# The split of the values moved from VectorE to GpSimd, from the third pair of heads on

## The chip, the cores and the metric

The kernel runs on one core of one Trainium2 chip. The metric is the time of one execution on the device in microseconds (us). Before the change the median of three runs is 1172.41 us (1171.74 to 1175.49).

A core has five engines, each with a queue of instructions of its own that it works off in order: TensorE (PE in the profile; PEld is its loading of weights), VectorE (DVE), ScalarE (ACT), GpSimd (POOL) and SyncE (SP), which here issues nearly all transfers (DMAs). Engines wait for one another by semaphores. SBUF is the memory on the core, with 128 partitions; PSUM is where TensorE puts its sums.

## The reference

Attention with pooled queries, then a mixture of experts in which each token goes to one expert. Cut to what matters:

```python
# q, k, v: (8, 8, 1152, 64) float32
q_pool = q.reshape(B, H, S // 2, 2, D).mean(axis=3)          # 576 queries
scores = (1 / np.sqrt(D)) * q_pool @ k.transpose(0, 1, 3, 2)
scores = scores - scores.max(-1, keepdims=True)
attn = np.exp(scores)
attn = attn / (attn.sum(-1, keepdims=True) + 1e-9)
x = (attn @ v).transpose(0, 2, 1, 3).reshape(4608, 512)

logits = x @ w_gate + modality_bias[modality_id]             # 8 experts
e_idx = logits.argmax(1)
probs = softmax(logits)
for e in range(8):                                           # w1[e]: 512 x 1024, w2[e]: 1024 x 512
    mask = e_idx == e
    out[mask] = probs[mask, e][:, None] * (np.maximum(x[mask] @ w1[e], 0) @ w2[e])
```

## The kernel before

The 64 heads are worked on as 32 pairs: two batches of one head, one in the lower and one in the upper 64 partitions. To keep nearly float32 precision on float16 matrix products, each operand is split into a high part (the value rounded to float16) and a low part (the remainder, again float16), and products of the parts are summed in PSUM.

A loop runs over 576 steps, 18 for each pair. In each step a fixed string of letters says how much of each kind of work is put out: matrix products for the row maxima (`maxpass`, a pair ahead), scores and exponentials (`scores`), products of exponentials and values (`pv`). Everything that prepares a pair is put at a step relative to its first one, by constants such as `T_QH`, `T_VH` or `T_VL`. So the order of instructions on TensorE, VectorE, ScalarE and GpSimd is written out by hand (`MANUAL`). SyncE is not in that list: the order of its transfers is set by a planner when the program is made, from what it expects to be ready when.

What the engines do for a pair `p`, with the lines of the profile:

- *Queries and keys.* GpSimd adds the two queries of each pool (L613, `rawq<-rawq`), rounds them to `qh` (L620) and forms the remainders of queries and keys (L648, `lo`); ScalarE rounds the keys to `hi` (L632). SyncE then moves `qh` into `QB`, for the maxima, and `qh`, `lo` and `hi` into the operands `B` (L583), and loads the next `rawq`, `rawk` and `rawv` (L598, L599, L603).
- *Maxima.* TensorE multiplies `QB` and `hi` into `pm`, in one of three PSUM buffers (L781, L789); VectorE reduces each to its maximum (L782, L790), forms `m` (L753), TensorE turns it (L757), VectorE writes it as a row `mr` (L766), and SyncE moves the row into `B` (L767).
- *Scores.* TensorE makes the scores (L843, L844), ScalarE the exponentials as 32 bit words (`Pe`, L845). The upper halves of these words are the high parts; the lower halves are turned into the low parts `Pl` by ScalarE for two thirds (L826) and by VectorE for one (L828).
- *Values.* ScalarE sums the squares of the pair's values (L694), TensorE adds over the partitions (L700), and VectorE makes of it a power of two, the scale `sc` (L708). Then the function `values` runs four times a pair, with `PARTS` cutting nine chunks of 128 keys into five and four (640 and 512 columns). With `lo` false, GpSimd writes the scaled values, rounded to float16, into `VH` (L735); with `lo` true, VectorE computes value times scale minus `VH` into `vl` in one instruction (L733). Their steps are 15 and 14 ahead of the pair (the piece of 512 first) and 11 and 2 ahead. VectorE also makes `VS`, which is `VH` times 2^-16 (L745, 12 steps ahead). `VH` and `VS` have three buffers each, by the pair's number, and `vl` three.
- *Products.* TensorE multiplies `VH`, `vl` and `VS` with the parts of the exponentials into `xp` (L894, L895, L896). VectorE divides by the sums and writes `x` (L912, L913, L917). After each odd pair SyncE stores the 128 columns of the two (`xs<-x`, L218), and ScalarE and VectorE split them (L862, L869) for the logits.

The first two pairs differ: there GpSimd scales the values in place (L730) and subtracts (L731), after ScalarE has made `VH` (L737). After each eight pairs VectorE and GpSimd route the tokens of two batches (`route`); in the last pairs VectorE also makes the lists of tokens for the first expert blocks (`first_list`). After about 760 us come the expert layers, in which VectorE and ScalarE split the weights and GpSimd gathers and scatters tokens.

The function that the change touches and what calls it:

Of the kernel before, what the change touches and what calls it, by code (L numbers as in the profile page):

```python
# [16 lines left out]
ALU = mybir.AluOpType  # L17
# [62 lines left out]
QH_POOL = True  # L80
LO_POOL = (0, 1, 2)
VH_POOL = (0, 1)
EV_ACT = ()
IN_PM = (0, 1, 2, 3, 4, 5)
EVD = 1
# [463 lines left out]
def attention(tc, ctx, att, ident, npairs, xpool, on_two, on_split, on_scale, jobs, side, set_pm, started, ahead, hip):  # L549
# [3 lines left out]
    nc = tc.nc  # L553
# [25 lines left out]
    def need(p, *names):  # L579
        assert all((p, n) in made for n in names), f"pair {p}: {names} are not made yet"  # L580
# [137 lines left out]
    flat = lambda a: a.rearrange("p c j d -> p (c j) d")  # L718

    def values(p, i, lo):  # L720

        s = st[p]
        c = slice(*PARTS[lo][i:i + 2])
        made.add((p, f"v{'hl'[lo]}{i}"))
        if lo:
            need(p, f"vh{i}")
        v = flat(s["v"].rearrange("p (c j d) -> p c j d", c=NKC, j=2)[:, c])
        vh = flat(VH[p % 3][:, c, :, 0:D])
        if lo and p < 2:
            nc.gpsimd.tensor_scalar(v, v, s["sc"], None, op0=ALU.mult)  # L730
            nc.gpsimd.tensor_tensor(flat(s["vl"][:, c]), v, vh, op=ALU.subtract)  # L731
        elif lo:
            nc.vector.scalar_tensor_tensor(flat(s["vl"][:, c]), v, s["sc"], vh, op0=ALU.mult, op1=ALU.subtract)  # L733
        elif p > 1 and i in VH_POOL:
            nc.gpsimd.tensor_scalar(vh, v, s["sc"], None, op0=ALU.mult)  # L735
        else:
            nc.scalar.activation(vh, v, AF.Copy, scale=s["sc"])  # L737
# [283 lines left out]
    for p in range(npairs):  # L1021
        b = NSTEP * p
        go = lambda t, f, *a, p=p, b=b, **k: at(b + t, p, lambda: f(p, *a), **k)
        if p > 1:
            d = D2 if p == 2 else (0,) * 5
            go(T_K2 - b if p == 2 else T_KQ, load_kq, end=False)
            go(T_SPLIT + d[0], split_q)
            go(T_QH + d[1], split_qh)
            for i in range(2):
                go(T_HI[i] + d[2], split_hi, i)  # L1030
            for i in range(3 if LOC else 7):
                go(T_LO[LOCI[i] if LOC else i] + d[3], split_lo, i)
            go(T_MAX + d[4], lambda p: mxq.append(maxpass(p)), end=False)
            go(T_PLACE + (T_P2 if p == 2 else 0), place, end=False)
            go(T_LV, load_v)
        elif p:
            go(T_P1 - b, place, end=False)
            go(T_M1 - b, lambda p: mxq.append(maxpass(p)), end=False)
            go(T_LV, load_v)
        sq, power_, vh, vs, vl = (T_SQ, T_POW, T_VH, T_VS, T_VL) if p > 1 else V1 if p else V0  # L1040
        if p == 1:
            go = lambda t, f, *a, p=p: at(t, p, lambda: f(p, *a))
        go(sq, square)
        go(power_, power)
        for i, t in enumerate(vh):
            go(t, values, i, False)
        go(vs, shifted)
        for i, t in enumerate(vl):
            go(t, values, i, True)
# [15 lines left out]
    for t in range(NSTEP * npairs):  # L1065
        p, c18 = divmod(t, NSTEP)
# [422 lines left out]
```

## Time and profile before

The profile is one execution of the program, taken by the hardware profiler.

| What | Value |
|---|---|
| Median of three runs | 1172.41 us |
| The profiled execution's own time | 1171.42 us |
| Its span, first to last instruction | 1169.7 us |
| Busy: PE, DVE, ACT, POOL | 95%, 84%, 78%, 36% |
| Granted TensorE clock, mean | 0.996 |
| Products of values (L894), first and last start | 31.4 and 763.1 us |

How to read it: a row that names a line has engine, operation, what is written `<-` what is read, the shape, and how often (x). In a table of groups there follow the total busy time in us, the mean of one in ns, and the idle time of the engine just ahead of it with what ended it. In a view in order of time a row begins with the start and the length in us, and the bracket says how long the engine had been idle and for what it had waited; a row may merge neighbours of one form (x2). In a list of waits the three numbers are the total in us, how often, and the longest. A wait is put down to the semaphore that came last. Matrix products are pipelined and their ends modelled; the spans on POOL are rough.

### The profile page before, as it was taken

What the parts mean: (1) busy time and instruction counts of PE and PEld (TensorE: products, weight loads), DVE (VectorE), ACT (ScalarE), POOL (GpSimd) and SP (SyncE); (2) the same over time, 40 slices, a digit from 0 to 9 for tenths busy, and PEclk for the clock granted to TensorE, in tenths of its full rate; (3) what the DMA queues carried; (4) which work ended last, traced back from release to release, by engine and by line L of the source; (5) the groups of instructions that cost most, each with busy time, mean ns of one, the idle gap of its engine ahead of it and who ended that gap; (6) DMA issues with size and microseconds to landing.
All of it is one profiled execution on the core that took longest, in us unless ns stands there. A gap on an engine that the chain in (4) does not pass through costs nothing. (4 is left out here: it accounts for less than half of the span.)

```text
span 1169.7 us, 36628 instructions
## 1 busy us (share of the span) xinstructions
PE 1113.4 (95%) x14962; PEld 816.2 (70%) x14962; DVE 985.5 (84%) x2031; ACT 918.1 (78%) x1459; POOL 417.3 (36%) x393
## 2 busy tenths in 40 slices
PE   6989999999999999999999899999999999999995
PEld 2667777777777777777776677767667676676763
DVE  6898898999999999999999999888997757566661
ACT  5879999998999998999998888865466656566561
POOL 7743444444435344443444352123112121211200
PEclk9999999999999999999999999999999999999998
DMA  7667768767668678578577463499999999999970
GB/s 226 168 160 174 162 169 200 156 168 177 169 165 189 176 165 177 160 172 193 151 183 173 135 135 93 146 292 279 222 283 283 333 270 284 276 284 275 258 250 22
DMA packets 175569, 232.66 MB, mean 199 GB/s; under 512 B 92351, under 2 KB 126799, under 8 KB 175392
## 3 DMA queue, kind: packets, MB, share of 16 engines
q1 hardware_dynamic: 169254, 210.45, 69.4%
q0 software_dynamic: 6128, 19.78, 6.3%
q8 instruction: 119, 1.95, 0.7%
q14 instruction: 58, 0.48, 0.2%
q10 hardware_dynamic: 10, 0.00, 0.0%
HBM read 146.11 MB, written 19.18 MB: 141 GB/s over the span
## 5 line engine op out<-in xcount | busy, mean ns | idle before, releaser
L845 ACT ACTIVATE Pe<-psc 128x432 int32<-128x432 f32 x768 | 381.5, 527 | 65.1 <-PE psc L844 54.3
L782 DVE TENSOR_REDUCE mp<-pm 128x1 f32<-128x512 f32 x566 | 369.8, 683 | 13.7 <-PE pm L781 8.2
L894 PE MATMUL xp<-VH,Pe 128*128 128x65 f16 x2880 | 373.2, 193 | 0.0
L896 PE MATMUL xp<-VS,Pl 128*128 128x65 f16 x2880 | 372.6, 193 | 0.4 <-DVE Pl L828 0.4
L895 PE MATMUL xp<-vl,Pe 128*128 128x64 f16 x2880 | 371.3, 192 | 0.0
L895 PEld LDWEIGHTS <-Pe 128*128 128x128 f16 x2880 | 267.6, 98 | 87.8
L894 PEld LDWEIGHTS <-Pe 128*128 128x128 f16 x2880 | 272.1, 98 | 57.1 <-issue 19.4
L844 PE MATMUL psc<-B 65*128 65x432 f16 (+2 forms) x1152 | 306.7, 289 | 1.9 <-DMA B<-mr 1.8
L843 PE MATMUL psc<-B 128*128 128x432 f16 (+2 forms) x1152 | 306.0, 288 | 1.7 <-ACT Pe L845 1.7
L896 PEld LDWEIGHTS <-Pl 128*128 128x128 f16 x2880 | 266.4, 97 | 0.6 <-DVE Pl L828 0.5
L781 PE MATMUL pm<-hi,QB 128*128 128x512 f16 x566 | 215.4, 383 | 17.6 <-DVE mp L782 13.6
L826 ACT ACTIVATE Pl<-Pe 128x1152 f16<-128x1152 uint16 x186 | 216.5, 1164 | 5.9
L735 POOL TENSOR_SCALAR VH<-rawv,sc 128x512 f16<-128x512 f32 (+1 forms) x60 | 103.7, 1739 | 185.4 <-PE xp L896 125.4
L648 POOL TENSOR_TENSOR lo<-rawk,hi 128x576 f16<-128x576 f32 (+1 forms) x68 | 90.2, 1329 | 182.1 <-ACT hi L632 142.2
L1228 PE MATMUL ph<-xpart,w1h 128*128 128x256 f16 x544 | 148.3, 273 | 0.1
L1230 PE MATMUL ph<-xpart,w1l 128*128 128x256 f16 x544 | 148.3, 273 | 0.0
L1229 PE MATMUL ph<-xpart,w1h 128*128 128x256 f16 x544 | 148.3, 273 | 0.0
L844 PEld LDWEIGHTS <-B 65*128 65x128 f16 x1152 | 113.4, 98 | 25.8 <-issue 3.2
L843 PEld LDWEIGHTS <-B 128*128 128x128 f16 x1152 | 113.0, 98 | 9.0 <-issue 3.7
L828 DVE TENSOR_SCALAR Pl<-Pe 128x576 f16<-128x576 uint16 (+1 forms) x198 | 108.1, 546 | 8.5 <-ACT Pe L845 7.1
L1276 PE MATMUL po<-w2h,hl 128*128 128x512 f16 x296 | 112.2, 379 | 0.0
L1275 PE MATMUL po<-w2l,hh 128*128 128x512 f16 x296 | 112.2, 379 | 0.0
(263 smaller groups left out, 1790.6 us busy)
## 6 DMA issues: line engine op xcount, KB each, us to landing
w2r<-in_w_dram SPq DMA_DIRECT2D x76, 512.0 KB
w1r<-in_w_dram SPq DMA_DIRECT2D x72, 512.0 KB
rawv<-in_att_dram SPq DMA_DIRECT2D x32, 576.0 KB
B<-hi SPq DMA_DIRECT2D x128, 144.0 KB
rawq<-in_att_dram SPq DMA_DIRECT2D x31, 576.0 KB
rawk<-in_att_dram SPq DMA_DIRECT2D x31, 576.0 KB
B<-qh SPq DMA_DIRECT2D x128, 72.0 KB
B<-lo SPq DMA_DIRECT2D x64, 144.0 KB
```

The costliest lines, as they stand in the source:

```text
L781: nc.tensor.matmul(pm, QB[p % 2][:, u], s["hi"][:, t * 512:(t + 1) * 512], start=True, stop=True)
L782: nc.vector.tensor_reduce(mp[:, u, t:t + 1], pm, op=ALU.max, axis=AX.X)
L826: nc.scalar.activation(low, rest, AF.Copy, scale=LOW)
L843: nc.tensor.matmul(o, b1[:, ks], b1[:, qs], start=True, stop=False, skip_group_check=True)
L844: nc.tensor.matmul(o, b2[:, ks], b2[:, qs], start=False, stop=True, skip_group_check=True)
L845: nc.scalar.activation(Pe[:, D + x0:D + x1], pt, AF.Exp, scale=1.0 / 16)
L894: nc.tensor.matmul(out, Ph[:, qs], vh[:, c, j, 0:D + 1], start=c == 0 and g == 0, stop=False, skip_group_check=True)
L895: nc.tensor.matmul(out[:, 0:D], Ph[:, qs], vl[:, c, j], start=False, stop=False, skip_group_check=True)
L896: nc.tensor.matmul(out, Pl[:, qs], vs[:, c, j, 0:D + 1], start=False, stop=c == NKC - 1, skip_group_check=True)
L1228: nc.tensor.matmul(o, hi[:, c, fs], xh[:, :, c], start=c == 0, stop=False)
L1229: nc.tensor.matmul(o, hi[:, c, fs], xl[:, :, c], start=False, stop=False)
L1230: nc.tensor.matmul(o, lo[:, c, fs], xh[:, :, c], start=False, stop=c == 3)
```

## The change

From the third pair on (`VLP = 2`) `values` takes a new branch. With `lo` false, GpSimd multiplies the float32 values by the scale in place and then copies them to `VH`, which rounds them. With `lo` true, GpSimd subtracts `VH` from the scaled values and writes `vl`. The steps at which the function is called stay as they are; VectorE's instruction on L733 and GpSimd's on L735 are no longer reached.

```diff
+VLP = 2
...
         v = flat(s["v"].rearrange("p (c j d) -> p c j d", c=NKC, j=2)[:, c])
         vh = flat(VH[p % 3][:, c, :, 0:D])
-        if lo and p < 2:
+        if p >= VLP:
+            if lo:
+                nc.gpsimd.tensor_tensor(flat(s["vl"][:, c]), v, vh, op=ALU.subtract)
+            else:
+                nc.gpsimd.tensor_scalar(v, v, s["sc"], None, op0=ALU.mult)
+                nc.gpsimd.tensor_copy(vh, v)
+        elif lo and p < 2:
             nc.gpsimd.tensor_scalar(v, v, s["sc"], None, op0=ALU.mult)
             nc.gpsimd.tensor_tensor(flat(s["vl"][:, c]), v, vh, op=ALU.subtract)
         elif lo:
```

## The prediction

> **What bounds the kernel now.** I read the span on the page first, then the table of busy time by stretches, then who waited for whom on TensorE and VectorE, then the order of time of one pair, engine by engine.
>
> ```profile
> span 1169.7 us, 36628 instructions
> 60.00:560.00 500.00, 485.37 (x8333) 374.37 (x8331) 463.89 (x1041) 460.81 (x781) 217.17 (x175) 1.00 0.73 173
> 560.00:740.00 180.00, 168.72 (x2890) 129.39 (x2889) 173.07 (x420) 160.08 (x267) 66.58 (x53) 1.00 0.59 141
> 373.97:395.94 21.97, 21.97 (x390) 17.12 (x389) 21.46 (x48) 20.64 (x36) 9.68 (x7) 1.00 0.57 155
> ```
>
> The columns of the last three rows are the length, then busy PE, PEld, DVE, ACT, POOL, the granted clock and DMA. The change acts between 60 and 740 us. TensorE is idle there for 14.6 + 11.3 = 25.9 us, at a granted clock of 1.00. One whole pair (373.97 to 395.94) has TensorE busy from end to end: relieving VectorE gives nothing in such a pair. So the gain can come only from the idle time of TensorE. The next view says who ended it, first for 100 to 560 us, then for 560 to 740 us (total, times, longest).
>
> ```profile
> PE pm L781 <- DVE mp L782: 6.5, 10, 1.4
> PE pm L757 <- DVE m L753: 1.6, 3, 0.5
> ...
> PE pm L781 <- DVE mp L782: 6.1, 10, 1.0
> PE pm L757 <- DVE m L753: 2.5, 5, 1.0
> ```
>
> VectorE ends most of it: 8.1 us in the long middle and 8.6 us in the last seven pairs, where VectorE also makes the lists of tokens for the experts and is busy 173 of 180 us. These 16.7 us are the ceiling of a gain by VectorE. Part of the middle is no lack of VectorE at all, but a transfer that VectorE waits for, ahead of the maxima that TensorE needs:
>
> ```profile
> DVE x L917 <- DMA xs<-x: 18.5, 9, 2.9
> 411.90 0.55 DVE L917 SCALAR_TENSOR_TENSOR x<-xp,sc,rr 128x320 f32<-128x320 f32 x1 [2.06 <-DMA xs<-x]
> 413.10 0.38 PE L781 MATMUL pm<-hi,QB 128*128 128x512 f16 x1 [0.50 <-DVE mp L782]
> ```
>
> **The change, part by part.** VectorE loses two instructions in each of 30 pairs. GpSimd's two scalings turn into scalings in place, and gain two copies and two subtractions. The forms are all in the trace, some from the first two pairs, or at 576 columns:
>
> ```profile
> L733 DVE SCALAR_TENSOR_TENSOR vl<-rawv,sc,VH 128x640 f16<-128x640 f32 x30 | 28.3, 943 | 0.0
> L733 DVE SCALAR_TENSOR_TENSOR vl<-rawv,sc,VH 128x512 f16<-128x512 f32 x30 | 22.3, 744 | 0.0
> L730 POOL TENSOR_SCALAR rawv<-rawv,sc 128x640 f32<-128x640 f32 x2 | 4.1, 2038 | 7.7 <-ACT VH L737 4.5 <-issue 3.2
> L730 POOL TENSOR_SCALAR rawv<-rawv,sc 128x512 f32<-128x512 f32 x2 | 3.3, 1662 | 0.0
> L731 POOL TENSOR_TENSOR vl<-rawv,VH 128x640 f16<-128x640 f32 x2 | 2.9, 1460 | 0.2
> L731 POOL TENSOR_TENSOR vl<-rawv,VH 128x512 f16<-128x512 f32 x2 | 2.2, 1116 | 0.2
> L620 POOL CAST qh<-rawq 128x576 f16<-128x576 f32 x30 | 20.1, 670 | 0.1
> ```
>
> *Removed from VectorE*: 28.3 + 22.3 = 50.6 us, 1.69 us a pair.
>
> *Added to GpSimd*: the scalings in place cost 2.04 + 1.66 against 1.89 + 1.56 (the rows of one pair, below), so +0.25; two copies at 0.67 per 576 columns are 0.74 + 0.60; the subtractions are 1.46 + 1.12. Sum 4.17 us a pair, from 9.68 to 13.85 of 21.97 us. It has the room, but it is a queue in order, and here is where its pieces stand in one pair:
>
> ```profile
> 373.97 1.56 POOL L735 TENSOR_SCALAR VH<-rawv,sc 128x512 f16<-128x512 f32 x1 [5.58 <-PE xp L896]
> 375.51 1.89 POOL L735 TENSOR_SCALAR VH<-rawv,sc 128x640 f16<-128x640 f32 x1
> 377.34 0.67 POOL L620 CAST qh<-rawq 128x576 f16<-128x576 f32 x1
> 378.09 1.28 POOL L648 TENSOR_TENSOR lo<-rawq,qh 128x576 f16<-128x576 f32 x1
> 381.94 1.71 POOL L648 TENSOR_TENSOR lo<-rawk,hi 128x576 f16<-128x576 f32 x1 [2.57 <-ACT hi L632]
> 387.58 1.29 POOL L648 TENSOR_TENSOR lo<-rawk,hi 128x576 f16<-128x576 f32 x1 [3.93 <-ACT hi L632]
> 388.82 1.41 POOL L613 TENSOR_TENSOR rawq<-rawq 128x576 f32<-128x576 f32 x1
> ```
>
> After the change: scale, copy, scale, copy end at 373.97 + 1.66 + 0.60 + 2.04 + 0.74 = 379.0; the first subtraction at 380.5; `qh` at 381.1, 3.1 us later than now; the `q` remainder at 382.4; the first `k` remainder about 0.5 later than now (its wait of 2.57 takes up the rest); the second still waits for ScalarE; the second subtraction follows it and pushes the sum of the next queries by 1.12, to about 389.9. Nothing wants these early: the shifted copy `VS` at 380.66 (below) has its values at 379.0, a margin of 1.6 us; both remainders `vl` are ready at 380.5 and about 390.0, while VectorE now only starts them at 381.63 and 391.54. So I cost the lateness of `vh` and `vl` at nothing; the cover is that 1.6 us, and if a longer GpSimd used it up, VectorE would stall by the excess in each pair.
>
> *The shared access of VectorE and GpSimd.* Some VectorE instructions are stretched when a GpSimd instruction began shortly before:
>
> ```profile
> L828 DVE TENSOR_SCALAR Pl<-Pe x198: 436/454/1539, 23.7 to 761.8; 128x576 f16<-128x576 uint16 x186, 128x864 f16<-128x864 uint16 x12
> L828 DVE TENSOR_SCALAR Pl<-Pe 128x576 f16<-128x576 uint16 x186 | 100.9, 543 | 6.7 <-ACT Pe L845 5.5
> 375.70 0.92 DVE L828 TENSOR_SCALAR Pl<-Pe 128x576 f16<-128x576 uint16 x1
> 380.29 0.46 DVE L828 TENSOR_SCALAR Pl<-Pe 128x576 f16<-128x576 uint16 x1
> 380.66 0.46 DVE L745 TENSOR_SCALAR VS<-VH 128x1152 f16<-128x1152 f16 x1
> 381.63 0.88 DVE L733 SCALAR_TENSOR_TENSOR vl<-rawv,sc,VH 128x640 f16<-128x640 f32 x1
> 383.62 0.45 DVE L828 TENSOR_SCALAR Pl<-Pe 128x576 f16<-128x576 uint16 x1
> 390.51 0.45 DVE L828 TENSOR_SCALAR Pl<-Pe 128x576 f16<-128x576 uint16 x1
> 391.54 0.74 DVE L733 SCALAR_TENSOR_TENSOR vl<-rawv,sc,VH 128x512 f16<-128x512 f32 x1
> ```
>
> `Pl` takes 0.454 undisturbed, 0.543 in the mean, up to 1.539: 186 x 0.089 = 16.6 us are lost now, 0.55 a pair. By position, in the pair shown: the `Pl` at 375.70 (0.92, begun 0.19 after a scaling) will meet the copy begun at 375.6 instead, which ends at 376.2: 0 to 0.2 less. `Pl` and `VS` at 380.29 and 380.66, free now, meet the end of the subtraction, `qh` and the `q` remainder: 0 to 1.1 (the largest stretch seen), I take 0.4. `Pl` at 383.62, or a little earlier with `vl` gone ahead of it, meets the pushed `k` remainder: 0 to 0.7, taken 0.3. `Pl` at 390.51 meets the pushed sum of the queries: 0 to 0.7, taken 0.3. Together 0.9 a pair (-0.2 to 2.5). VectorE's net relief is 1.69 - 0.9 = **0.8 us a pair** (-0.8 to 1.9).
>
> [...]
>
> *The queue of SP.* `qh` 3.1 us later means that its two transfers into `QB` are issued later. SP's order is not written by hand; the planner sets it. An ordinary pair, then one in which routing made `qh` late:
>
> ```profile
> 400.01 1.10 SPq L583 DMA_DIRECT2D QB<-qh  x2
> 401.21 0.53 SPq L603 DMA_DIRECT2D rawv<-in_att_dram  x1
> 401.84 0.39 SPq L598 DMA_DIRECT2D rawq<-in_att_dram  x1
> 402.33 0.39 SPq L218 DMA_DIRECT2D xs<-x  x1
> ...
> 447.32 0.38 SPq L218 DMA_DIRECT2D xs<-x  x1
> 450.67 1.41 SPq L583 DMA_DIRECT2D QB<-qh  x2
> ```
>
> In the ordinary pair the store `xs<-x` stands behind `QB`, `rawv` and `rawq`; it is the store for which VectorE waits at 411.90. Where `qh` is late, the planner put the store ahead of `QB`, and it goes out 3 us before it. I expect that order everywhere after the change: the store then goes out up to 2.3 us earlier (402.33 less 400.01, the issues that stand ahead of it now), and ahead of the load of `rawq`. Of VectorE's nine waits (2.06 each) most should go, and with them the stalls of TensorE behind them, like the 0.50 above. Bounds: nothing gained, or 3 us lost each (second rival).
>
> **The sum.** The last stretch: seven pairs of 0.8 would be 5.6, of the 8.6 there I take 4.5. The middle: 8.1 us of stalls, of which I take 2.5, for the store and for the pairs with routing together. 4.5 + 2.5 = 7 us. The profiled execution took 1171.4 us (1.7 outside its span): 1171.4 - 7 = 1164.4. The median of the runs shown is 1.0 above it, so **1165 us**, 0.6% faster. The experts' stage, from about 760 us, has none of the changed lines and is taken as it is.
>
> **The rivals.** (1) *Given back at the shared access*: new meetings cost 1.7 to 2.2 us a pair, inside the bounds above, and VectorE ends where it was, or 0.5 a pair worse. For it: four of its instructions stand just where GpSimd's new ones fall, and the stretch of 1.08 exists. Against it: most `Pl` are at 0.454, though GpSimd is busy 44% of a pair. Time: 1172, or with 5 pairs x 0.5 in the last stretch 1174.5. [...] (2) *The store behind the late `QB`*, the slower side: if SP keeps the order of the ordinary pair, the store goes out at 405.4 instead of 402.33, VectorE's wait of 2.06 becomes 5.1, and TensorE stalls 3 us more in each of nine pairs: 27 us, 1199. It decides as soon as the store is some 0.8 us later (9 x 0.8 = 7). Against it stands the order at 447.32. (3) *All of VectorE's stalls go*: -16.7, 1156; for it, VectorE falls from 21.46 to 20.7 in a pair of 22; against it, the listing work comes in bursts that 0.8 us do not cover.
>
> **How the numbers follow.** Forecast (4 to 13 us faster) 0.50; (1) 0.29; (2) whole or in part 0.14; (3) 0.07. A measurement of this kernel tells about 0.3% (3.5 us) from no change: faster 0.57, same 0.26, slower 0.17 (a few hundredths of (1) end slower). The range of 1156 to 1180 reaches past both ends of (1) to a part of (2), takes in the edge of (3) and leaves out the rest of these two; the forecast's own is 1159 to 1169.
>
> **What would show it.** Right: line 733's work gone from VectorE; GpSimd near 13.85 us a pair; the mean of `Pl` between 0.55 and 0.70; the store ahead of `QB` on SP; VectorE's wait for `xs<-x` well under 18.5 us; TensorE's idle time from 560 to 740 us at 6 to 8 us. Wrong: `Pl` and `VS` stretched by over 1.7 us a pair; a longer wait for `xs<-x`; VectorE waiting for `VH` ahead of `VS`; or stalls of TensorE that stay though VectorE is freer.

## The result and the profile after

The change makes the kernel **slower by 1.3%**: 1187.51 us (median of six runs, 1182.51 to 1190.86) against 1172.08 us (six runs, 1169.38 to 1175.49) of the kernel before on the same chip, ratio 1.0126 [1.0094, 1.0159]. Measured again on another chip it was 1.0215 [1.0184, 1.0247]. I had forecast 1165 us and a range up to 1180. Lines beyond `values` have moved by seven, lines ahead of it by one: L782 of before is L789, L917 is L924, L583 is L584.

The span, and the mean granted clock of the core, before (first row) and after:

```profile
core 0: 1169.7 us, clock 0.996
```
```profile
core 0: 1187.7 us, clock 0.990
```

Busy time by stretches (length, then PE, PEld, DVE, ACT, POOL, granted clock, DMA), the attention stage cut at 560 us. Before:

```profile
60.00:560.00 500.00, 485.37 (x8333) 374.37 (x8331) 463.89 (x1041) 460.81 (x781) 217.17 (x175) 1.00 0.73 173
560.00:760.00 200.00, 187.69 (x3260) 145.35 (x3259) 189.67 (x459) 177.62 (x300) 71.72 (x57) 1.00 0.58 145
```

After:

```profile
60.00:560.00 500.00, 477.63 (x8141) 367.48 (x8138) 444.60 (x968) 449.90 (x761) 295.02 (x262) 0.99 0.70 167
560.00:760.00 200.00, 183.68 (x3124) 141.58 (x3121) 185.12 (x435) 171.66 (x289) 104.38 (x91) 0.98 0.59 140
```

VectorE is freer, as intended (463.9 to 444.6), GpSimd does more (217 to 295), and TensorE does *less*: its idle time grows from 14.6 + 12.3 to 22.4 + 16.3 us, by 11.8, and it also runs at a lower clock. The clock lost 0.4% of a span of 1169.7 before and 1.0% of 1187.7 after, 7.2 us more. Together 19 us, about the 18.0 by which the span grew; the windows are fixed, so the sum is rough. The last product of values starts at 781.3 instead of 763.1, 18.2 us later, so the loss lies in the attention stage.

Who ended TensorE's idle time between 60 and 760 us (total, times, longest). Before:

```profile
PE pm L781 <- DVE mp L782: 12.6, 20, 1.4
PE pm L757 <- DVE m L753: 5.3, 9, 1.2
PE psc L844 <- DMA B<-mr: 0.9, 3, 0.4
```

After, with VectorE's own wait for the store, which before was 18.5 us (nine times, 2.9 at most; the prediction's row holds for 60 to 760 us too):

```profile
PE pm L788 <- DVE mp L789: 27.5, 30, 3.2
PE pm L764 <- DVE m L760: 3.8, 7, 1.4
PE psc L851 <- DMA B<-mr: 1.3, 2, 1.0
```
```profile
DVE x L924 <- DMA xs<-x: 30.6, 10, 4.4
```

So TensorE waits 15 us longer for the maxima, from an engine that was relieved of 50 us (23 net of the stretches listed below), and that engine waits 12 us longer for the store. The two belong together: summed over TensorE's rows in order of time, 60 to 760 us, all its waits for maxima and for `m` are 21.3 us before and 34.6 after, and those that begin within 2 us behind a wait of VectorE for the store are 4.6 and 15.9. Of the 13.3 us more, 11.3 stand there. One ordinary pair after the change, in order of time; GpSimd's first scaling begins at 403.76. First `qh` on GpSimd, then SyncE's queue, VectorE and TensorE:

```profile
403.76 1.56 POOL L734 TENSOR_SCALAR rawv<-rawv,sc 128x512 f32<-128x512 f32 x1 [4.59 <-PE xp L903]
...
410.22 0.90 POOL L621 CAST qh<-rawq 128x576 f16<-128x576 f32 x1
...
411.14 1.10 SPq L584 DMA_DIRECT2D QB<-qh  x2
412.60 0.33 SPq L599 DMA_DIRECT2D rawq<-in_att_dram  x1
413.03 0.40 SPq L219 DMA_DIRECT2D xs<-x  x1
...
410.52 0.92 DVE L752 TENSOR_SCALAR VS<-VH 128x1152 f16<-128x1152 f16 x1
...
417.76 0.19 DVE L920 RECIPROCAL rr<-rs 128x5 f32<-128x5 f32 x1
421.36 0.55 DVE L924 SCALAR_TENSOR_TENSOR x<-xp,sc,rr 128x320 f32<-128x320 f32 x1 [3.40 <-DMA xs<-x]
...
422.56 0.38 PE L788 MATMUL pm<-hi,QB 128*128 128x512 f16 x1 [1.82 <-DVE mp L789]
```

`QB` goes out 7.4 us after the first scaling (before: 400.01 less 395.94, 4.1), and the store **still behind it**, at 9.3 instead of 6.4. VectorE waits 3.40 us instead of 2.06, and TensorE, which needs the maxima queued behind that wait, stalls 1.82 instead of 0.50. From its issue to VectorE's use the store took less time than before (413.03 to 421.36 is 8.3 us; 402.33 to 411.90 was 9.6), so 2.9 us of lateness became 1.3 us of stall. What followed this stall stands in the next view, stretches right behind it:

```profile
422.50:424.00 1.50, 1.44 (x21) 0.94 (x21) 1.50 (x5) 0.00 (x0) 0.00 (x0) 0.76 0.72 147
424.00:427.50 3.50, 3.50 (x37) 2.37 (x36) 2.37 (x5) 2.66 (x5) 0.00 (x0) 0.61 0.98 289
427.50:430.00 2.50, 2.50 (x51) 1.92 (x48) 1.87 (x9) 2.19 (x4) 0.98 (x1) 1.00 1.03 281
```

The granted clock fell to 0.76 and then 0.61 in these stretches, and in 3.5 us TensorE works off 37 products, where 51 fit into the next 2.5: (0.24 x 1.5) + (0.39 x 3.5) = 1.7 us lost, on top of 1.8 us of stall. Between 60 and 760 us there are four such stretches, 6.8 us in all, each with the clock at 0.50, and none in before: two follow stalls behind the store (2.86 and 1.82 us), two follow stalls of 3.15 and 2.43 us near the end of the stage that do not stand behind it.

What the moved and the touched instructions cost after (busy us, mean ns):

```profile
L734 POOL TENSOR_SCALAR rawv<-rawv,sc 128x640 f32<-128x640 f32 x30 | 61.4, 2046 | 0.0
L735 POOL CAST VH<-rawv 128x640 f16<-128x640 f32 x30 | 21.4, 714 | 2.0
L735 POOL CAST VH<-rawv 128x512 f16<-128x512 f32 x30 | 18.7, 623 | 1.9
L732 POOL TENSOR_TENSOR vl<-rawv,VH 128x640 f16<-128x640 f32 x30 | 40.7, 1358 | 2.5
L732 POOL TENSOR_TENSOR vl<-rawv,VH 128x512 f16<-128x512 f32 x30 | 33.6, 1119 | 0.0
L621 POOL CAST qh<-rawq 128x576 f16<-128x576 f32 x30 | 25.6, 854 | 0.1
L835 DVE TENSOR_SCALAR Pl<-Pe 128x576 f16<-128x576 uint16 x186 | 114.9, 618 | 7.3 <-ACT Pe L852 6.1
L752 DVE TENSOR_SCALAR VS<-VH 128x1152 f16<-128x1152 f16 x31 | 27.6, 889 | 1.2 <-ACT VH L744 1.2
```

GpSimd's pieces take what I had taken for them. VectorE's `Pl` grew by 618 - 543 = 75 ns in 186 (14.0 us) and `VS` from 0.46 to 0.89 us in 31 (13.3 us): 27 us, 0.9 a pair.

### The profile page after: what moved, and what is told of

Same layout as the page of the kernel before. It is cut to its first block, busy times and chain, and to the rows that moved or that the text cites. A ratio compares the mean times of both kernels' runs of the same rounds, so it can differ in the third digit from the quotient of the medians.

```text
span 1187.7 us, 36751 instructions
## 1 busy us (share of the span) xinstructions
PE 1118.6 (94%) x14962; PEld 820.0 (69%) x14962; DVE 976.5 (82%) x1971; ACT 916.7 (77%) x1459; POOL 534.6 (45%) x513
## 5 line engine op out<-in xcount | busy, mean ns | idle before, releaser
L789 DVE TENSOR_REDUCE mp<-pm 128x1 f32<-128x512 f32 x566 | 367.5, 681 | 20.2 <-PE pm L788 12.2
L734 POOL TENSOR_SCALAR rawv<-rawv,sc 128x512 f32<-128x512 f32 (+1 forms) x60 | 108.3, 1805 | 158.5 <-PE psc L851 71.3
L649 POOL TENSOR_TENSOR lo<-rawk,hi 128x576 f16<-128x576 f32 (+1 forms) x68 | 83.9, 1237 | 119.3 <-ACT hi L633 66.3
L835 DVE TENSOR_SCALAR Pl<-Pe 128x576 f16<-128x576 uint16 (+1 forms) x198 | 122.1, 617 | 9.0 <-ACT Pe L852 7.7
L850 PEld LDWEIGHTS <-B 128*128 128x128 f16 x1152 | 113.4, 99 | 14.4 <-issue 9.2
L1292 POOL DMA_INDIRECT out_dram<-o,siB x25 | 28.4, 1138 | 202.8 <-ACT o L1289 167.5
```

Of the source, the lines that this page charges most:

```text
L789: nc.vector.tensor_reduce(mp[:, u, t:t + 1], pm, op=ALU.max, axis=AX.X)
L850: nc.tensor.matmul(o, b1[:, ks], b1[:, qs], start=True, stop=False, skip_group_check=True)
```

## The experiments

Each ratio is to the kernel before, measured beside it on the same chip; before takes between 1170 and 1181 us on the chips used, so ratios are compared and not times, but for runs of one chip (1 to 4, 5 to 8, 9 to 12, 13 to 16). Two explanations stand against each other: the **store** (the late `qh` holds SyncE's queue, and VectorE waits for the store) and the **shared access** (GpSimd's longer work stretches VectorE's instructions). The second name stands for what the traces show and no more: a VectorE instruction beside GpSimd's work can take longer, as the `Pl` of 0.92 us in before that takes 0.45 elsewhere. Most expectations call them theory A and theory B.

### Taking the wait away: two buffers for x

```diff
-            xts[p] = xts[p - 1] if p % 2 else xpool.tile([P, NT, 2 * D], F32, name="x2")
+            xts[p] = xts[p - 1] if p % 2 else xpool.tile([P, NT, 2 * D], F32, name="x2", bufs=2)
```

Run 1:

> The changed kernel with two buffers for the attention output x, so that VectorE need not wait for the store xs<-x of the pair before. Theory A (the late qh holds up SyncE's queue, the store goes out at 9.3 instead of 6.4 us after the first scaling, VectorE waits for it, TensorE stalls behind): the 15 us of TensorE idle time at that place go and the drops of the granted clock with them, so 1168 to 1174 us, clock 0.996. Theory B (VS and Pl are stretched at the shared access with GpSimd, ahead of the maxima): nothing changes but the wait, VectorE keeps its stretches, 1182 to 1188 us.

Measured: 1.0212 [1.0156, 1.0267], no better than the change itself (1.0126 and 1.0215 on two other chips). Neither number that I had written was met. VectorE's wait for the store is gone, but TensorE's waits from 60 to 760 us now begin with the row of maxima:

```profile
PE psc L851 <- DMA B<-mr: 21.2, 10, 4.0
PE pm L788 <- DVE mp L789: 11.8, 20, 3.2
```

The stall had only been hidden behind the first one. The row goes out on SyncE's queue behind the late `QB`, the store and two transposes that wait for the freshly split `x`. Taking one waiter away left the lateness in the queue, and the next in line paid (21.2 us). The late `QB` alone doesn't make the row late: in run 9 below `QB` is as late, the store is off the queue, and the row goes out 14.4 to 15.4 us after the first scaling in the nine pairs in which before waits for the store, where it is 16.7 to 17.4 here.

### Lateness alone, relief alone

Two runs on the kernel before. One makes `qh` late without the change, by two fills on GpSimd ahead of it:

```diff
         if p > 1:
+            for _ in range(2):
+                nc.gpsimd.memset(idle, 0.0)
             (nc.gpsimd if QH_POOL else nc.vector).tensor_copy(qh, s["q"][:, 0:SQ])
```

Run 3:

> The kernel before with two memsets of 1800 float16 columns on GpSimd ahead of qh, about 3.1 us, and nothing else changed: VectorE keeps its instruction for the low part. Theory A: the store goes out later by about 2 us, VectorE's wait for it grows from 18.5 to 30 us or more, TensorE stalls, 1180 to 1188 us. Theory B: the memsets read nothing from SBUF and VectorE is hardly stretched, 1171 to 1175 us.

Measured: 1.0244 [1.0203, 1.0284]. VectorE keeps its old work here, and the loss is at least as large as the change's (up to 1.0215). TensorE's waits, from 60 to 760 us:

```profile
PE pm L784 <- DVE mp L785: 16.8, 38, 2.8
PE psc L847 <- DMA B<-mr: 10.3, 10, 1.5
PE pm L760 <- DVE m L756: 8.5, 8, 3.9
PE pm L784 <- DMA QB<-qh: 5.6, 3, 4.7
```

Four waits share it, and the store is hardly among them: VectorE waited 9.2 us for it, half of before's. The pushed `qh` and the pushed remainder behind it also meet `VS` (862 ns in the mean) and one `vl` (1226 for 943), so it isn't a pure delay.

The other takes the relief without its price; it leaves out the low parts of the values from the third pair on, so that VectorE does without L733 and GpSimd is as before:

```diff
         elif lo:
-            nc.vector.scalar_tensor_tensor(flat(s["vl"][:, c]), v, s["sc"], vh, op0=ALU.mult, op1=ALU.subtract)
+            pass
```

Run 4:

> The kernel before without the low parts of the values from the third pair on (VectorE's instruction is left out and nothing stands in its place, so vl holds the squares). It prices VectorE's relief of 1.69 us a pair by itself. My prediction's sum: up to 16.7 us could go, about half of it should, 1160 to 1167 us. The rival that a freer VectorE runs into the wait for the store in any case: 1168 to 1172 us.

Measured: 0.9955 [0.9929, 0.9981], 5 us for a relief of 50.6. VectorE mostly waits earlier for what comes next (60 to 760 us):

```profile
DVE mp L782 <- PE pm L781: 30.5, 49, 2.5
DVE x L917 <- DMA xs<-x: 25.8, 10, 3.5
```

It doesn't reach the store sooner: in the ordinary pairs the wait begins up to 7.5 us behind the store's issue, as in before. The wait is longer because the store took longer on this chip, 8.8 to 10.5 us from issue to use in the ten waits against 8.4 to 9.7; a second trace of before, below, waits 25.7 us without any change. The 7 us that I had put on a net relief of 0.8 us a pair were more than the whole relief of 1.69 is worth.

### Earlier or less late: qh and the subtractions moved

Four runs move GpSimd's pieces about. The first keeps the change and puts `qh` and the queries' remainder earlier; in the program they then stand between the first copy and the second scaling:

```diff
+T_QE = -33
...
-            go(T_QH + d[1], split_qh)
+            go((T_QH if p == 2 else T_QE) + d[1], split_qh)
...
-                go(T_LO[LOCI[i] if LOC else i] + d[3], split_lo, i)
+                go((T_QE if i == 0 and p > 2 else T_LO[LOCI[i] if LOC else i]) + d[3], split_lo, i)
```

Run 2:

> The changed kernel with GpSimd's rounding of the queries (qh) and their remainder put right behind the sum of the queries, ahead of the scalings, instead of behind them. Theory A: QB no longer waits for GpSimd, the store goes out at about 5 us after the first scaling, VectorE's wait for it is under 5 us in all, 1166 to 1174 us. Theory B: GpSimd does the same work at other places, some stretches move, 1180 to 1188 us.

Measured: 0.9994 [0.9973, 1.0016]. Hardly a wait for the store is left in the trace (0.2 us), and the loss is gone, but no gain comes: `VS` now waits for `VH` and is stretched further in the mean, and TensorE stalls 0.8 us behind it in eleven pairs; its waits for maxima and `m` are 30.0 us in all.

```profile
DVE VS L753 <- POOL VH L736: 6.1, 10, 0.6
```
```profile
L753 DVE TENSOR_SCALAR VS<-VH 128x1152 f16<-128x1152 f16 x31 | 31.4, 1013 | 7.9 <-POOL VH L736 6.7 <-ACT VH L745 1.2
```

So the margin of 1.6 us ahead of `VS`, which the prediction named as the cover of a late `VH`, is real, and this run uses it up. The same edit on the kernel before (one step earlier, right behind the queries' sum):

Run 5:

> The kernel before with qh and the queries' remainder right behind the sum of the queries on GpSimd, a good 5 us ahead of the scalings; no other change. SyncE's planner then puts the store xs<-x ahead of the transfers of qh into QB. Theory A (SyncE's queue, held up by a late qh, passes its lateness to the store and to the row of maxima): VectorE's wait for the store falls from 18.5 to under 8 us, ratio to the kernel before 0.994 to 0.998. Theory B (only the shared access of VectorE and GpSimd matters): 0.998 to 1.003.

Measured: 1.0013 [0.9994, 1.0032], no gain, and in the range written for the shared access. The wait for the store fell to 8.6 us, but VectorE's two `vl` met the moved pieces, 1030 and 1007 ns instead of 943 and 744: 10.5 us in thirty pairs. The third adds to the change both the early `qh` and a first subtraction four steps later:

```diff
-T_VL = (-11, -2)
+T_VL = (-7, -2)
+T_QE = -34
```

Run 6:

> The changed kernel with qh and the queries' remainder ahead of the scalings, and the first subtraction behind the first remainder of the keys (T_VL -7 instead of -11), so that VS meets no subtraction. Theory A alone: no wait for the store, ratio 0.990 to 0.997. Theory B alone: GpSimd does the same work and stretches VectorE as much, 1.005 to 1.015. Both (A for the transfers, B for what is left): 0.992 to 1.000, with VS back near 0.46 us.

Measured: 1.0037 [1.0010, 1.0063]. `VS` is back at 455 ns, but the planner put SyncE's transfers in another order, and the store went out 7.0 to 9.3 us after the first scaling all the same: VectorE waited 20.5 us for it. None of the three ranges that I had written was met. Bringing `qh` forward doesn't help where the store doesn't come with it.

### One half of the change at a time

Only the scaling in place and the copy on GpSimd; the remainders stay on VectorE, as a plain subtraction:

```diff
-                nc.gpsimd.tensor_tensor(flat(s["vl"][:, c]), v, vh, op=ALU.subtract)
+                nc.vector.tensor_tensor(flat(s["vl"][:, c]), v, vh, op=ALU.subtract)
```

Run 8:

> The high part of the change alone: GpSimd scales in place and copies, VectorE subtracts. qh is late by about 1.6 us, half of the change's lateness, and VectorE is not relieved. Theory A: the store goes out 1 to 1.5 us later, 1.002 to 1.010. Theory B: only the two copies are new on GpSimd and they fall where no Pl stands, 0.999 to 1.003.

Measured: 1.0071 [1.0051, 1.0090]. Here `qh` is 1.6 us late, and the store's wait is only 6.0 us; another part stands out, the subtraction of 640 columns on VectorE:

```profile
L732 DVE TENSOR_TENSOR vl<-rawv,VH 128x640 f16<-128x640 f32 x30 | 35.7, 1190 | 0.0
```

It takes 1190 ns where the fused form took 943, though the same subtraction of 512 columns took 682, less than the fused 744: some 0.3 us of it is by that, in my estimate, a meeting with GpSimd (682 x 640 / 512 = 853). In one pair it began at 407.24, 0.18 us behind GpSimd's remainder, and took 1.77 us, and TensorE stalled 0.90 us at 409.7; nine pairs have such a stall of 0.9. TensorE waited 19.0 us for the maxima (12.6 in the first trace of before), none of it right behind a wait for the store. So the shared access can cost by its place, without the store. The other half keeps GpSimd's scaling into `VH` as it was, and forms the remainders on GpSimd, late, by a scaling in place and a subtraction as in the first two pairs:

```diff
-T_VL = (-11, -2)
+T_VL = (-7, -2)
...
-        if p >= VLP:
+        if lo:
+            nc.gpsimd.tensor_scalar(v, v, s["sc"], None, op0=ALU.mult)
+            nc.gpsimd.tensor_tensor(flat(s["vl"][:, c]), v, vh, op=ALU.subtract)
+        elif p > 1 and i in VH_POOL:
+            nc.gpsimd.tensor_scalar(vh, v, s["sc"], None, op0=ALU.mult)
```

Run 7:

> GpSimd keeps its scaling into VH as before the change and takes over the low parts alone, with a scaling in place and a subtraction in each piece, the first piece behind the first remainder of the keys (step -7), so qh is not late at all, and VectorE is freed of the same 1.69 us a pair. Theory A: 0.994 to 1.000, the store goes out at 6.4 us after the first scaling as before. Theory B: GpSimd works 1.9 us a pair more than in the change, so at least the same loss, 1.010 to 1.020.

Measured: **0.9955 [0.9934, 0.9975], faster than before**, with *more* work on GpSimd than the change has. Nothing stands ahead of `qh` that didn't before, and VectorE's wait for the store is 1.7 us in all. That wait is below the 18.5 us of before for two other reasons: the load of `rawv` no longer stands ahead of the store, which goes out at about 5.9 us instead of 6.4, and VectorE comes to it later, because its split of `x` (L867; L869 in before) takes 1362 ns in the mean instead of 810. Its stretch from 60 to 560 us, and its group of `Pl`:

```profile
60.00:560.00 500.00, 488.38 (x8405) 377.15 (x8402) 467.06 (x1000) 462.68 (x785) 346.98 (x264) 1.00 0.73 175
```
```profile
L826 DVE TENSOR_SCALAR Pl<-Pe 128x576 f16<-128x576 uint16 x186 | 116.4, 626 | 7.8 <-ACT Pe L843 6.6
```

GpSimd is busy 347 of 500 us (295 after the change), `Pl` is as stretched as there (626 against 618), and TensorE has 11.6 us of idle time where the changed kernel has 22.4. TensorE's waits for maxima and `m` that don't stand behind the store are 17.9 us (16.7 in before), so the gain over before came with the store's wait; no gain of VectorE's relief is seen in them.

### The store on another queue

The store moved to ScalarE's queue, on the changed kernel, on the one before and on the last one; `NPAIR // 2 - 1` is the store that was on GpSimd's queue already:

```diff
-            rt.store(g, cc, x2, eng)
+            rt.store(g, cc, x2, nc.gpsimd if n == NPAIR // 2 - 1 else nc.scalar)
```

Run 9:

> The changed kernel; the stores xs<-x (but the one of the last pairs of heads of the first half) are issued by ScalarE's queue instead of SyncE's, so that they no longer stand behind the two transfers QB<-qh. Theory A (what the change lost it lost at the store alone: 11 us of stalls of TensorE at nine places and 6.8 us of half clock behind them): the store goes out at about 4 us after the first scaling, VectorE's wait for it falls from 30.6 us to under 6, no other wait grows by more than 4 us, and the time is 0.990 to 0.999 of before, as I had predicted for a store ahead of QB. Theory B (the lateness belongs to everything behind QB on SyncE's queue): the wait for the store goes, but TensorE's wait for the row of maxima (1.3 us now) grows beyond 8 us, as in the run with two x2, and the time is 1.003 to 1.02.

Measured: **0.9902 [0.9870, 0.9934]**. With SyncE no longer between them, VectorE doesn't wait for the store at all, TensorE's wait for the row of maxima didn't grow, and its waits from 60 to 760 us are:

```profile
PE psc L850 <- ACT Pe L852: 12.1, 19, 1.7
PE pm L788 <- DVE mp L789: 6.2, 8, 1.7
...
ACT Pe L852 <- DVE x L924: 13.4, 4, 3.4
```

The first is the price of the place: ScalarE has to wait for `x` before it can issue the store, and TensorE for ScalarE, 0.6 us in each odd pair. This is my forecast's condition, a store that isn't behind `QB`, and the loss is gone with it, though `VS` still took 909 ns and `Pl` 628. How much of the 0.990 is the change's own, the next run tells.

Run 11:

> The kernel before, with the stores xs<-x on ScalarE's queue. Theory A (VectorE's wait for the store, 18.5 us in nine pairs, costs TensorE the 3.9 us of stalls that follow it): that wait falls under 5 us and the time is 0.995 to 0.999. Theory B (the wait only takes the place of others, TensorE is busy from end to end in such a pair): 0.999 to 1.003, TensorE idle for as long as before; an issue on ScalarE, which is busy 92% of the time, could add 0.2 us a pair of heads and so 3 us, at most 1.003.

Measured: 0.9942 [0.9920, 0.9965], a little below the lowest value that I had written. The kernel before loses time to this store too: the planner's place for it costs 0.6% without any change. Beside it on the same chip, run 9 (1169.59 us) is 0.3% under run 11 (1173.45): that is what the change is worth once the store is out of the way of both, about what run 4 gave for the whole relief. A difference of 0.3% is at the edge of what can be told here (run 14).

Run 12:

> The kernel of the seventh run (GpSimd scales into VH as before the change, and forms the remainders late by a scaling in place and a subtraction), which took 0.9955, with the stores xs<-x on ScalarE's queue. Its wait for the store was 1.7 us already, so if the store was the only reason the two kernels differ from the changed one, nothing changes: 0.993 to 0.998. If shorter SyncE queues are worth something by themselves: 0.988 to 0.993.

Measured: 0.9944 [0.9922, 0.9965], as without the move (0.9955 on another chip), where hardly a wait for the store was left to remove (1.7 us), and as run 11 without the relief (0.9942): in this form the relief is worth nothing.

### The dose, on one chip

The change with nothing but the first subtraction four steps later, so that `qh` is 1.6 us late and not 3.1:

```diff
-T_VL = (-11, -2)
+T_VL = (-7, -2)
```

Run 10:

> The changed kernel with the first subtraction of a pair four steps later in the program (behind the q remainder and the first k remainder on GpSimd), so that qh is 1.6 us later than before the change and no longer 3.1. All other work of the change stays. Theory A (lateness of the store sets the price): the store goes out about 1.6 us later than before the change, VectorE's wait for it is between 18.5 and 30 us, the stalls of TensorE behind it about half of the 15 us, at most one drop of the clock: 1.000 to 1.006. Theory B (the shared access of VectorE and GpSimd sets the price): it stays at 1.009 to 1.016.

Measured: 0.9908 [0.9874, 0.9942], better than both theories had it. On that chip before takes 1181 us, so the comparison was run again beside the changed kernel and before themselves:

Run 13:

> The changed kernel unedited, beside the next three on one chip. Theory A (qh too late on SyncE's queue makes the loss): it stays slower than before, 1.005 to 1.016, and over 1.2% slower than the kernel with the late subtraction. Theory B (the loss came from the chip of the first comparison): 0.993 to 1.003.

Run 14:

> The kernel before, unedited, with a trace of its own on this chip: 0.998 to 1.002 of its other runs. If the chip is one on which before takes about 1180 us, the trace has to show 8 to 10 us that the first trace of before does not: theory A, as more and longer waits for the store and half-clock stretches behind them; theory B, in the stage of the experts or the start.

Run 15:

> The tenth run's kernel again (the changed kernel with the first subtraction behind the q remainder and the first k remainder). Theory A: 0.987 to 0.998, and 1.2% to 2.2% under the changed kernel of this call. Theory B (0.991 was the chip): 0.998 to 1.006, at most 0.5% under the changed kernel.

Run 16:

> The kernel of the run before this one, with the stores xs<-x on ScalarE's queue too. Theory A (what is left of the loss, 6 stalls of 1 to 2.3 us at 17 us after a pair's first scaling, comes from the store alone): another 0.4 to 1.0% faster than with the late subtraction alone. Theory B (one edit is enough, ScalarE's issue stalls TensorE 0.6 us in each odd pair instead): within 0.4% of it.

| Kernel, one chip | Median us | Ratio to before |
|---|---|---|
| changed | 1200.22 | 1.0215 [1.0184, 1.0247] |
| before, a second time | 1179.79 | 1.0027 [1.0002, 1.0053] |
| changed, first subtraction late | 1170.82 | 0.9957 [0.9935, 0.9980] |
| the same, store on ScalarE's queue | 1165.39 | **0.9913 [0.9883, 0.9942]** |

The second row is the same program against itself and misses 1 by 0.3%: differences of that size aren't told apart here. The others are: **moving one subtraction behind `qh` takes the changed kernel from 2.2% slower to 0.4% faster**, and the store's move 0.5% further; this is the fastest of the four. The first two miss what I had written (1.005 to 1.016, and 0.998 to 1.002), the first by more; the other two lie in theory A's ranges against before, though the third is 2.4% under the changed kernel and I had 1.2 to 2.2. The third kernel had 0.9908 on the chip of run 10, so ratios from two chips can differ by 0.5%. Here are the waits from 60 to 760 us of the four. The changed kernel, then before:

```profile
PE pm L788 <- DVE mp L789: 31.2, 30, 3.5
...
DVE x L924 <- DMA xs<-x: 34.3, 10, 5.1
```
```profile
PE pm L781 <- DVE mp L782: 19.6, 22, 2.3
...
DVE x L917 <- DMA xs<-x: 25.7, 9, 3.8
```

With the subtraction late, with VectorE's two stretched groups; then with the store on ScalarE's queue too:

```profile
PE pm L788 <- DVE mp L789: 18.1, 26, 2.1
...
DVE x L924 <- DMA xs<-x: 22.6, 9, 3.7
```
```profile
L835 DVE TENSOR_SCALAR Pl<-Pe 128x576 f16<-128x576 uint16 x186 | 130.0, 699 | 5.9 <-ACT Pe L852 4.6
L752 DVE TENSOR_SCALAR VS<-VH 128x1152 f16<-128x1152 f16 x31 | 14.0, 451 | 1.2 <-ACT VH L744 1.2
```
```profile
PE psc L850 <- ACT Pe L852: 12.0, 18, 1.7
PE pm L788 <- DVE mp L789: 5.0, 7, 1.0
```

Between the first and the third kernel, VectorE is stretched by the same amount: 186 x (699 - 543) = 29 us in the third against 14.0 + 13.3 = 27 after the change. The wait for the store falls by 11.7 us, TensorE's wait for maxima by 13.1, and the span from 1190.9 to 1168.4. So it is not the sum of the stretches that makes the loss. Nor is it the place of `VS` by itself, which is free again in the third kernel: run 9 has it stretched (909 ns) and no loss. TensorE's waits right behind a wait for the store fall from 19.5 to 8.6 us, 10.9 of the 14.8 us by which its waits for VectorE's maxima and `m` fall.

The trace of before on this chip answers the other question: the same program waits 25.7 us for the same store instead of 18.5, and TensorE 19.6 us for the maxima instead of 12.6. That is 7 of the 10.1 us by which this span (1179.8) exceeds the first one. The rest was not followed further.

## Why the prediction was wrong

*What held.* VectorE lost its 50.6 us. GpSimd's added pieces came out as taken (2.05 against 2.04 for the larger scaling, 0.71 and 0.62 against 0.74 and 0.60 for the copies, 1.36 against 1.46 for the larger subtraction). The stretches were 0.9 us a pair, the value taken, though `VS` had a larger part of it (0.43) than I gave it together with one `Pl` (0.4). `qh` came 3.3 us later (7.4 against 4.1), predicted 3.1. VectorE did not wait for GpSimd's `VH`, nor TensorE for `vl`. The experts' stage is unchanged (406.6 us from the last product of values to the end before, 406.4 after).

*The step that failed* is the one on **the queue of SP**: "I expect that order everywhere after the change: the store then goes out up to 2.3 us earlier". It went out 2.9 us later, in the order of the ordinary pair (`QB`, `rawq`, store); only the load of `rawv` moved away. I had one row, the store at 447.32 ahead of `QB` at 450.67, from a pair with routing, and took a rule from it for pairs without. The list of a queue is fixed when the program is made, and a planner that foresaw a late `qh` in one case needn't do so in the other. In the trace of before all nine pairs in which VectorE waits have `QB` first, and only the three pairs with routing have the store first; after the change the same three do. The ordinary pairs were the nearer rows. With the store off that queue the changed kernel came out at 0.990 of before (run 9), where the forecast had 0.994; but before with the same move came out at 0.994 (run 11), so the change itself gave 0.3% there, half of the forecast.

*The rival that came true* is the second, the store behind the late `QB`, to which I gave 0.14. Its mechanism and place were right, and its price was a term too large and a term short. 3 us a place, 27 us, measured 1.3 us in the pair shown and 15 us more in TensorE's wait for maxima (27.5 against 12.6, all places): the later store took 1.2 us less to its use in the pair shown, and VectorE came to it 0.3 us later. The half clock (0.50 granted) behind four stalls of 1.82 to 3.15 us, 7 us in all (half of it behind the store), I had not foreseen.

*The first rival*, everything given back at the shared access, is refuted as the cause of the 1.3%: stretches of 27 to 29 us a run stand in the changed kernel (1.0215) and in the one with the late subtraction (0.9957) alike. The 1.7 to 2.2 us a pair that it put on the new meetings no run shows; after the change it was 0.9, as above. That the place of a stretch can cost is shown by the run with the high parts alone (1.007) and by the one with `qh` early (0.9994), where TensorE stalls behind a late `VS`. In the pair shown `VS`, 0.46 us when alone, took 0.92: it began 0.30 into `qh` and ended at 411.44, 0.32 after `qh` did. The `Pl` at 375.70 in the prediction took 0.92 too, but ended 0.78 before the scaling beside it (375.51 + 1.89 = 377.40), so the end of GpSimd's instruction alone doesn't tell how long a stretch lasts.

*The value of the relief* was too high as well. Taking all of L733 away gave 0.45%, 5 us; the prediction had 7 us for less than half of it. The ceiling of 16.7 us of stalls was read rightly. In run 4's trace TensorE's waits for maxima and `m` that don't stand behind the store are 8.0 us (16.7 in before, 60 to 760 us), but those right behind it are 10.3 (4.6 in before, 11.6 in its second trace), and four stretches at half clock are there that neither trace of before has (granted clock 0.990 over the span, 0.996 in both of those). So the relief reaches VectorE's own stalls and not those at the store; what made the rest of the difference, on another chip, wasn't separated.

*What stays open*: VectorE waits about as long for the store in run 6 (20.5 us, ratio 1.004) as in run 15 (22.6 us, ratio 0.996), and as before: that wait alone doesn't rank kernels that are close to each other. What tells those two apart, the chip or the pieces' places, wasn't separated. The changed kernel was not tried with the store ahead of `QB` on SyncE's own queue.

## What to carry to other kernels

Before giving an engine more work, follow each queue that it feeds: here `QB`, issued 3.3 us later, put the store listed behind it 2.9 us later, and who waited for *that* set the price, not the engine's share of busy time (GpSimd busy 295 of 500 us at a ratio of 1.0126, 347 at 0.9955 in run 7). Take the order of a queue from the rows of the same kind of stage, and don't count on a planner to change it. Where such work must move, put the new pieces behind the one that feeds the queue: here the place of one subtraction was worth 2.5%, and the whole relief of VectorE 0.4%.

## What the runs showed of the hardware

- **The clock fell after a stall of 1.82 us.** It was followed, 0.7 us later, by 3.4 us at half clock (granted 0.50 in rows of half a microsecond, 0.61 in the row of 3.5 us), 1.7 us of work lost. It isn't certain: in the same trace no fall came after the stall of 1.81 us that ended at 516.91, and in the second trace of before the longest stall was 2.3 us, and the clock stayed at 1.00 in all its stretches of 100 us from 60 to 760. What decides it isn't shown.
- **Lateness moved along a queue.** With the store's wait removed by a second buffer (run 1), 21.2 us of waiting turned up at the row of maxima, which stands behind it on SyncE's queue, where the changed kernel had 1.3; with the store on ScalarE's queue (run 9) the list of TensorE's waits, down to 0.2 us, has none for that row.
- **A transfer's time differed from trace to trace.** The store of 576 KB took 9.2 us from issue to use in the mean of its nine waits in before, 8.2 in the ten of the changed kernel, and 9.9 in the second trace of before, on another chip; the last makes 6 of the 7 us by which that trace waits longer (25.7 against 18.5). Why wasn't tested: in before the load of `rawv`, 576 KB too, is issued 1.1 us ahead of the store, in the changed kernel it is elsewhere.
